# Float16 high and low parts in the MLP of an attention-plus-MLP kernel, from the third group on

## The chip, the core and the metric

The kernel runs on one core of a Trainium2 chip. Its time is that of one execution on the device in microseconds (us). The engines are named as in the profile: PE is TensorE (matrix products, with PEld its weight loads), DVE VectorE, ACT ScalarE, POOL GpSimd, and SP SyncE, which issues all transfers here.

## The reference

```python
# q, k, v: (8, 8, 576, 64); q and k about 0.67 in size, v 0.1
scores = 1/8 * q @ k^T;  rel = row - column
scores = where(0 <= rel < 128, scores - slope[head] * rel, -1e9)
attn   = softmax(scores);  y = attn @ v
x = y with the heads side by side: (4608, 512)
h = x @ w_in            # w_in: (512, 2048)
g = h / (1 + exp(-h))
out = g @ w_out         # w_out: (2048, 512)
```

q, k, v and out are float32, the weights float64. The kernel keeps close to float32 by splitting each MLP operand into a high and a low part and summing three products: high by high, high by low, low by high.

## The kernel before, in words

The 4608 rows are 36 blocks `i` of 128; a block has two passes `p` of four heads each. Two of the reference's batches make one of the kernel's four batches of nine blocks, with one scale for v. Four blocks are a group of 512 rows, nine groups `g`, counted from 0. While PE does the MLP of group g, it also does the attention of the next group's rows.

The order is written out by hand. A position counts half-slices of the MLP: the slice `f` of a group (16 of them, 128 of the 2048 columns each; `n` = 16 g + f) is two halves of the first product (`gemm1`, tile h) and two of the second (`gemm2`, tile o), so a group has 64 positions. Twelve matmuls of 512 columns belong to each product of a slice. The second product runs one slice behind the first. `put(position, function)` adds work to a position; all engines take their instructions in that order, each in its own queue. `at(p)` is the position at which pass p begins (`scores`); after it come `row_max`, `exps`, `p_hi` and `p_lo` (which split the softmax's numerator), a transposing transfer (`hl`), 13 to 15 positions later `attend`, and then `normalize`, `x_hi` and `x_lo`, which leave x as float16 high and low parts.

Between the products stand `act1` (ACT, tanh), `act2` (DVE), `act3` (ACT, gh: the high part) and `act4` (gl: the low part; POOL, and DVE in a group's last slice). MLP operands are float32r. x comes back through a transposing transfer (`x_dma`, tile xt, float16), and at the end of a group `turn_over` has `x_parts` write it out as float32r xh (ACT) and xl (DVE), 512 columns at a time. In group 0 ACT and DVE also split the float64 weights into high and low float32r parts (`w_split1` to `w_lo`). `vscale_load` and `vscale_reduce` find the largest |v| of the next batch, and `vscale_finish` turns it into a power of two: a reduction on DVE, a transpose on PE, small operations on one row, and a broadcast matmul on PE.

PSUM tiles of scores and of the attention's result share two buffers (`a`), so an `attend` waits until `row_max` has read scores of the buffer it takes.

Of the kernel before, what the change touches and what calls it, by code (L numbers as in the profile page):

```python
# [6 lines left out]
F32 = mybir.dt.float32  # L7
# [61 lines left out]
def tile_window_attention_then_silu_mlp(ctx, tc, qk, v, w_in, w_out, base8, out):  # L69
# [9 lines left out]
    ones16 = const.tile([P, 2 * P], BF16, name="ones16")  # L79
# [5 lines left out]
    def weight(kind, f):  # L85

        key = f"{kind}{f}"
        if key not in weights:
            shape = [P, NCC, P] if kind in ("wih", "wil") else [P, DM]
            if key in LAST:  # L90
                weights[key] = pool.tile(shape, F32R, tag=key, bufs=1, name=key)
            else:
                weights[key] = const.tile(shape, F32R, name=key)
# [27 lines left out]
    def keep_warm(n):  # L121

        for _ in range(n):
            nc.tensor.matmul(
                spare["a"][:, 4 * (D + 1) :], ones16[:, :P], ones16[:, : DM - 4 * (D + 1)],
                start=True, stop=True, skip_group_check=True,
            )

# [11 lines left out]
    def vscale_reduce(b, i):  # L140
        t = vred[b][i]
        if i == 0:
            vred[b]["m"] = pool.tile([P, VCH], F32, tag="vm", name=f"vmx{b}")
        m = vred[b]["m"][:, i : i + 1]
        if b == 0 and i < GT:
            rvs[i] = t

        if b == 0 and i % 2:
            nc.vector.tensor_reduce(m, t, axis=AX.X, op=ALU.max, apply_absolute_value=True)
        else:  # L150
            junk = pool.tile([P, DM], F32, tag="gt", name=f"vj{b}_{i}") if b == 0 else t
            nc.scalar.activation(junk, t, AF.Abs, accum_out=m)

    def vscale_finish(b, stage):
        r = vred[b]
        if stage == 0:
            r["col"] = col = pool.tile([P, 3], F32, tag="vcol", name=f"vcol{b}")
            nc.vector.tensor_reduce(col[:, 0:1], r["m"], axis=AX.X, op=ALU.max)
        elif stage == 1:
            col = r["col"]  # L160
            ps = ps_of(next_tag("misc"), f"vt{b}")
            nc.tensor.transpose(ps[:1, :P], col[:, 0:1], ident)
            c = col[:1, 1:2]
            nc.vector.tensor_reduce(c, ps[:1, :P], axis=AX.X, op=ALU.max)
# [4 lines left out]
            nc.vector.tensor_scalar(c.bitcast(I32), c.bitcast(I32), -1, 268 << 23, op0=ALU.mult, op1=ALU.add)
        else:  # L170
            ps = ps_of(next_tag("misc"), f"vs{b}")
            nc.tensor.matmul(ps[:, 0:2], ones[:1, :], r["col"][:1, 1:3], start=True, stop=True)
            vsc[b] = pool.tile([P, 2], F32, tag="vsc", bufs=3, name=f"vsc{b}")
            nc.vector.tensor_copy(vsc[b], ps[:, 0:2])
            del vred[b]


    ks, qs, rvs, st = {}, {}, {}, {}
# [190 lines left out]

    def x_dma(i):  # L370

        if i % 2 == 0:
            xt[i, "t"] = pool.tile([P, 2, 2 * NCC, P], F16, tag="big", name=f"xt{i}")
        nc.sync.dma_start_transpose(xt[i & -2, "t"][:, i % 2], xt[i].rearrange("p a c -> p (a c)"))

# [39 lines left out]

    def act3(n):
        gt = gact[n]
        gh = pool.tile([P, TG], F32R, tag="gh", name=f"gh{n}")
        gl = pool.tile([P, TG], F32R, tag="gl", name=f"gl{n}")
        nc.scalar.copy(gh, gt)  # L420
        gact[n] = (gh, gl, gt)

    def act4(n):
        gh, gl, gt = gact[n]
        (nc.vector if n % NF == NF - 1 else nc.gpsimd).tensor_sub(gl, gt, f32(gh))  # L425
# [16 lines left out]
    def gemm2(n, half):  # L442
        g, f = divmod(n, NF)
        for ti in (2 * half, 2 * half + 1):
# [4 lines left out]
            hi, lo = weight("woh", f), weight("wol", f)  # L449
            seq = [(gh, hi), (gh, lo), (gl, hi)]  # L450
            for i, (a, w) in enumerate(seq):
                nc.tensor.matmul(  # L452
# [2 lines left out]
                )  # L455

    def store(g, ti):
        tag, bufs = ("x", 4) if g == NG - 1 or ti > 1 else ("io", 2)
        ot = pool.tile([P, DM], F32, tag=tag, bufs=bufs, name=f"ot{g}_{ti}")
        if ti % 2:  # L460
            nc.vector.tensor_scalar_mul(ot, ops[ti], 0.5 / W_SCALE**2)
        else:
            nc.scalar.mul(ot, ops[ti], 0.5 / W_SCALE**2)
        nc.sync.dma_start(out[g * TG + ti * P : g * TG + (ti + 1) * P, :], ot)


# [47 lines left out]
    for p in range(NPAIR):  # L514
# [42 lines left out]
        if q == 0:  # L557
# [4 lines left out]
                put(n - 2, load_v, i)  # L562
            put(a - 3, v_hi, i)
            put(a - 2, v_lo, i)
    for b in range(1, NBB):
        n = at(2 * NBLK * b)
        for i in range(VCH):
            put(n - 54 + 5 * i, vscale_load, b, i)
            put(n - 50 + 5 * i, vscale_reduce, b, i)
        for x in range(3):  # L570
            put(n - 6 + 2 * x, vscale_finish, b, x)

    pos = [at(0)]

# [29 lines left out]
            fn(*a)  # L604

    with tc.manual_schedule():
        nc.gpsimd.memset(ones16, 1.0)
        nc.gpsimd.memset(ones, 1.0)
        make_identity(nc, ident)
# [105 lines left out]
```

## Time and profile before

| what | value |
|---|---|
| runs | 1033.23, 1029.6, 1031.43 us; median 1031.43 |
| the profiled execution | 1031.76 us, span 1030.0 us, mean granted PE clock 0.986 |
| busy: PE, DVE, ACT, POOL | 987.2, 572.2, 463.2, 217.9 us |
| chain that ended last | PE 79%, DVE 10%, transfers 4% |
| mean of `act1` (L409), `act2` (L414), `act3` (L420), `act4` on POOL (L425) | 597, 686, 615, 1310 ns |
| mean of a 512-column matmul from start to end | 395 to 414 ns (they overlap) |

A row of the timeline is start, duration, engine, line, operation, out<-in, shapes, count, and in brackets the idle time of the engine just before it with what ended it. A group's row has the count, then busy time and mean in ns, then idle time before. A row of a window has its length, then busy time and count of PE, PEld, DVE, ACT and POOL, the granted clock, the share of the transfer engines and GB/s.

### The profile page before, as it was taken

Reading aid. Unit: us, or ns where it says so; the run is one execution under the profiler, and the core shown is the slowest. Engines: PE = TensorE matmul, PEld = TensorE weight load, DVE = VectorE, ACT = ScalarE, POOL = GpSimd, SP = SyncE. Lnnn points to the kernel's source line nnn. Section 1 sums busy time; section 2 is a strip of 40 time slices with the busy share of each in tenths; the row PEclk is TensorE's granted clock in tenths of the full one; section 3 lists DMA queues with packets and bytes.
Section 4 is the critical chain, followed back from the end, with each engine's and each line's share of the span. In section 5 each row is a group of like instructions: output and inputs, shape, how many; then the busy total and the mean of one; then the engine's idle time right before and its main releaser. Section 6 shows DMA issues by size and latency. Waiting matters only on the chain.

```text
span 1030.0 us, 16885 instructions
## 1 busy us (share of the span) xinstructions
PE 987.2 (96%) x6374; PEld 782.8 (76%) x6374; DVE 572.2 (56%) x1399; ACT 463.2 (45%) x968; POOL 217.9 (21%) x188
## 2 busy tenths in 40 slices
PE   7978898999999998999999999999999999999998
PEld 5756676777777776777777778777777777787886
DVE  4889998555555555555555555554655555543111
ACT  4666676334454445334443355433444453333222
POOL 3022222122212221222122211222122212222221
PEclk8999999899999999999999999999999999999999
DMA  7278987333353446433353336433433444321001
GB/s 229 69 188 197 252 219 208 84 75 79 82 116 85 100 113 152 82 62 83 76 120 76 90 102 154 102 72 72 107 79 77 78 123 82 59 35 52 1 1 41
DMA packets 201073, 104.92 MB, mean 102 GB/s; under 512 B 168224, under 2 KB 176416, under 8 KB 200992
## 3 DMA queue, kind: packets, MB, share of 16 engines
q1 hardware_dynamic: 200992, 103.84, 42.7%
q8 instruction: 50, 0.82, 0.3%
q14 instruction: 31, 0.25, 0.1%
HBM read 54.00 MB, written 9.44 MB: 62 GB/s over the span
## 4 chain that ended last, share of the span: by engine, by line
PE 79%; DVE 10%; DMA 4%; issue 3%; ACT 2%; SPq 1%; POOL 0%; ACTq 0%; DVEq 0%; POOLq 0%
PE h L402 34%; PE o L452 32%; PE sp L227 6%; PE av L317 4%; DMA wr<-w_in 2%; DVE wm L492 2%; DVE t L247 1%; DVE wm L487 1%; DMA vm<-v 1%; DVE xl L390 1%; DVE hr L271 1%; DVE gt L414 1%; DVE wol L506 1%; DVE wil L506 1%; PE pt L289 1%
## 5 line engine op out<-in xcount | busy, mean ns | idle before, releaser
L425 POOL TENSOR_TENSOR gl<-gt,gh 128x512 fp32r<-128x512 f32 x135 | 176.9, 1310 | 776.4 <-ACT gh L420 683.5
L409 ACT ACTIVATE gt<-h 128x512 f32<-128x512 f32 x144 | 85.9, 597 | 445.3 <-PE h L402 445.2
L414 DVE SCALAR_TENSOR_TENSOR gt<-gt,h 128x512 f32<-128x512 f32 x144 | 98.8, 686 | 268.3 <-ACT gt L409 268.3
L402 PE MATMUL h<-xh,wih 128*128 128x512 f32 x576 | 238.2, 414 | 4.8 <-ACT xh L367 3.8
L452 PE MATMUL o<-woh,gh 128*128 128x512 f32 x576 | 230.9, 401 | 1.4 <-ACT gh L420 1.4
L452 PE MATMUL o<-woh,gl 128*128 128x512 f32 x576 | 229.9, 399 | 2.0 <-POOL gl L425 1.9
L452 PE MATMUL o<-wol,gh 128*128 128x512 f32 x576 | 228.4, 397 | 0.0
L402 PE MATMUL h<-xl,wih 128*128 128x512 f32 x576 | 227.5, 395 | 0.2 <-DVE xl L368 0.2
L402 PE MATMUL h<-xh,wil 128*128 128x512 f32 x576 | 227.6, 395 | 0.0
L271 DVE SCALAR_TENSOR_TENSOR hr<-t,hr 128x512 f16<-128x512 f32 (+1 forms) x128 | 121.0, 945 | 75.4 <-ACT hr L266 75.0
L402 PEld LDWEIGHTS h<-xh,wih 128*128 128x128 f32 x576 | 108.6, 189 | 32.6 <-ACT xh L367 4.0
L452 PEld LDWEIGHTS o<-woh,gl 128*128 128x128 f32 x576 | 109.0, 189 | 29.9 <-POOL gl L425 3.7
L452 PEld LDWEIGHTS o<-woh,gh 128*128 128x128 f32 x576 | 109.4, 190 | 27.0 <-ACT gh L420 2.3
L452 PEld LDWEIGHTS o<-wol,gh 128*128 128x128 f32 x576 | 109.3, 190 | 25.8
L402 PEld LDWEIGHTS h<-xh,wil 128*128 128x128 f32 x576 | 108.9, 189 | 25.0
L402 PEld LDWEIGHTS h<-xl,wih 128*128 128x128 f32 x576 | 109.0, 189 | 20.5 <-DVE xl L368 0.5
L257 ACT ACTIVATE t<-t,mx 128x256 f32<-128x256 f32 (+1 forms) x288 | 120.6, 487 | 7.3 <-DVE mx L247 7.0
L420 ACT CAST gh<-gt 128x512 fp32r<-128x512 f32 x144 | 88.5, 615 | 53.6 <-DVE gt L414 51.8
L247 DVE CUSTOM_DVE_ANT_0 t<-sp,tab 128x256 f32<-128x256 f32 (+1 forms) x288 | 101.5, 404 | 14.8 <-PE sp L227 8.4
L357 DVE TENSOR_TENSOR x<-xs,x 128x256 f16<-128x256 f32 x64 | 74.3, 1160 | 48.7 <-ACT x L351 48.7
L227 PEld LDWEIGHTS sp<-k,q 64*128 64x128 f32 x1088 | 68.5, 190 | 27.0 <-issue 26.1
L317 PEld LDWEIGHTS <-hl 128*128 128x128 f16 x1632 | 55.4, 98 | 38.9 <-issue 34.6
(68 smaller groups left out, 681.4 us busy)
## 6 DMA issues: line engine op xcount, KB each, us to landing
q<-qk SPq DMA_DIRECT2D x36, 256.0 KB, 3.0
k<-qk SPq DMA_DIRECT2D x36, 256.0 KB, 3.2
vm<-v SPq DMA_DIRECT2D x36, 256.0 KB, 3.7
out<-ot SPq DMA_DIRECT2D x36, 256.0 KB, 2.8
wr<-w_in SPq DMA_DIRECT2D x16, 512.0 KB, 4.0
wr<-w_out SPq DMA_DIRECT2D x16, 512.0 KB, 3.9
rv<-v SPq DMA_DIRECT2D x32, 256.0 KB, 3.0
hl<-hr SPq DMA_TRANSPOSE x128, 3.1
```

The lines of the kernel that those rows point to most:

```text
L227: nc.tensor.matmul(sp[h][:, u, o], qs[i][rows, 2 * q + u], ks[i - 1 + o][rows, 2 * q + u], start=True, stop=True, skip_group_check=True,)
L247: nc.vector.tensor_tensor_reduce(out=t[:, h, 2 * P - n :], in0=st[p]["sp"][h][:, u, o].rearrange("p o c -> p (o c)"), in1=tab[:, 4 * q + 2 ...
L257: nc.scalar.activation(x, x, AF.Exp, bias=st[p]["mx"][:, 2 * u + h : 2 * u + h + 1], scale=-1.0)
L271: nc.vector.scalar_tensor_tensor(out=hr[:, 1], in0=t[:, :, 2 * P - n :], scalar=PSCALE, in1=hr[:, 0], op0=ALU.mult, op1=ALU.subtract)
L317: nc.tensor.matmul(av[:, 2 * u + h, : rhs.shape[-1]], lhs, rhs, start=(n == 0), stop=(n == len(seq) - 1), skip_group_check=True,)
L357: nc.vector.tensor_sub(xt[i][:, 1, cols], st[p]["x"], xt[i][:, 0, cols])
L402: nc.tensor.matmul(hps[n], w[:, cc], x, start=(half == 0 and i == 0), stop=(half == 1 and i == len(seq) - 1), skip_group_check=True,)
L409: nc.scalar.activation(gt, hps[n], AF.Tanh, scale=0.5 / W_SCALE)
L414: nc.vector.scalar_tensor_tensor(out=gt, in0=gt, scalar=1.0, in1=hps[n], op0=ALU.add, op1=ALU.mult)
L420: nc.scalar.copy(gh, gt)
L425: (nc.vector if n % NF == NF - 1 else nc.gpsimd).tensor_sub(gl, gt, f32(gh))
L452: nc.tensor.matmul(ops[ti], a[:, t], w, start=(f == 0 and i == 0), stop=(f == NF - 1 and i == len(seq) - 1), skip_group_check=True,)
```

## The change

From group 2 on the first product, and from group 3 on the second, take float16 high and low parts instead of float32r.

- Weights: `w_stat` (ACT, one square with a sum for each of 32 weight tiles, positions 66 to 97) and `vscale_finish` (now also for weights, positions 100 to 102) give one power of two for each product; `conv1` (ACT), `conv2` and `conv3` (DVE) write each weight tile's float16 parts, w_in at positions 106 to 168, w_out at 172 to 234.
- x: `gemm1` moves the columns of the transposed tiles xt straight into PE, in group 2 from two tiles (two matmuls of 256 columns), later from one (512 columns). `x_parts` stays for groups 0 and 1 alone. `x_unit` makes one scale for a group with rows of two batches.
- gh and gl: `act3` scales by 2^-25 to float16; `act4` is on DVE in these groups. `act1` and `store` take their scale from a tile (`mlp_scales`).
- Maxima of v: for batches 1 to 3 all on DVE (before on ACT), and earlier: finished at positions 52 to 54, 180 to 182 and 308 to 310 (before 60 to 64, 204 to 208, 348 to 352).
- The matmuls that keep PE's clock up before the MLP take the identity instead of ones.

```diff
+IN16, OUT16 = 2, 3
+CUT = 2.0**-25
+STATS, CONV_IN, CONV_OUT = 66, 106, 172
...
-        if b == 0 and i % 2:
+        if b > 0 or i % 2:
             nc.vector.tensor_reduce(m, t, axis=AX.X, op=ALU.max, apply_absolute_value=True)
...
+    def w_stat(which, f):
...
+        nc.scalar.activation(
+            junk, f32(w_parts(f, which)[0]), AF.Square, accum_out=vred["w", which]["m"][:, f : f + 1]
+        )
...
+        if n // NF >= IN16:
+            g, w = n // NF, w16[0, f]
+            for cc in (2 * half, 2 * half + 1):
+                seq += [(0, 0, cc), (0, 1, cc), (1, 0, cc)]
+            for i, (wp, xp, cc) in enumerate(seq):
...
+                c = xp * NCC + cc
+                if g > IN16:
+                    moves = [(hps[n].rearrange("p (t c) -> p t c", t=GT), xt[g, "g"][:, :, c])]
+                else:
+                    moves = [
+                        (hps[n][:, k * P : (k + 2) * P].rearrange("p (t c) -> p t c", t=2), xt[g * GT + k, "t"][:, :, c])
+                        for k in (0, 2)
+                    ]
+                for k, (o, x) in enumerate(moves):
+                    nc.tensor.matmul(o, w[:, wp, cc], x, start=start and k == 0, stop=stop, skip_group_check=True)
+            return
...
+        if n // NF >= OUT16:
+            nc.vector.scalar_tensor_tensor(out=gl, in0=gt, scalar=CUT, in1=gh, op0=ALU.mult, op1=ALU.subtract)
+            return
         (nc.vector if n % NF == NF - 1 else nc.gpsimd).tensor_sub(gl, gt, f32(gh))
...
-        more = n // NF + 1 < NG
+        more = n // NF + 1 < IN16
...
-        tag, bufs = ("x", 4) if g == NG - 1 or ti > 1 else ("io", 2)
+        tag, bufs = ("x", 4) if ti > 1 else ("io", 2)
...
+        nc.scalar.activation(out16, f32(hi), AF.Copy, scale=wsc["w", which][:, 0:1])
...
+        r = pool.tile([P, DM], F32, tag="io", name=f"wr16_{which}_{f}")
...
+        nc.vector.scalar_tensor_tensor(
+            out=r, in0=f32(hi), scalar=wsc["w", which][:, 0:1], in1=out16, op0=ALU.mult, op1=ALU.subtract
+        )
...
+            out=low16, in0=f32(w_parts(f, which)[1]), scalar=wsc["w", which][:, 0:1], in1=r, op0=ALU.mult, op1=ALU.add
...
+    for k in range(2 * NF):
+        put(STATS + k, w_stat, k % 2, k // 2)
+    for x in range(3):
+        for which in range(2):
+            put(STATS + 2 * NF + 2 + x, vscale_finish, ("w", which), x)
+    for which, n in enumerate((CONV_IN, CONV_OUT)):
+        for f in range(NF):
+            for k, fn in enumerate((conv1, conv2, conv3)):
+                put(n + SLICE * f + (k if which or f else 0), fn, which, f)
...
-        n = at(2 * NBLK * b)
+        n = at(2 * GT * (NBLK * b // GT)) + 2
         for i in range(VCH):
             put(n - 54 + 5 * i, vscale_load, b, i)
             put(n - 50 + 5 * i, vscale_reduce, b, i)
         for x in range(3):
-            put(n - 6 + 2 * x, vscale_finish, b, x)
+            put(n + x, vscale_finish, b, x)
```

Three places in the engines' queues follow, each as it stood before and as it stands now; a row is line, operation, out<-in.

ACT in group 1, slices 23 and 24 in the program's count (gt and gh are `act1` and `act3`, t is `exps`, hr is `p_hi`), before:

```order
L409 ACTIVATE gt23_2778<-h23_2758 128x512
L257 ACTIVATE t21_0_2765<-t21_0_2765,mx21_2756 128x256 x2
L257 ACTIVATE t21_1_2781<-t21_1_2781,mx21_2756 128x256 x2
L266 ACTIVATE hr21_0_2796<-t21_0_2765 128x512
L420 CAST gh23_2798<-gt23_2778 128x512
L266 ACTIVATE hr21_1_2809<-t21_1_2781 128x512
L409 ACTIVATE gt24_2854<-h24_2813 128x512
```

ACT at the same slices now (wj is `w_stat`):

```order
L487 ACTIVATE gt23_2836<-h23_2814 128x512
L308 ACTIVATE t21_0_2821<-t21_0_2821,mx21_2810 128x256 x2
L163 ACTIVATE wj0_13_2844,stat0_2388<-wih13_1951 128x512
L308 ACTIVATE t21_1_2839<-t21_1_2839,mx21_2810 128x256 x2
L317 ACTIVATE hr21_0_2856<-t21_0_2821 128x512
L163 ACTIVATE wj1_13_2858,stat1_2402<-woh13_2084 128x512
L500 CAST gh23_2860<-gt23_2836 128x512
L317 ACTIVATE hr21_1_2871<-t21_1_2839 128x512
L163 ACTIVATE wj0_14_2875,stat0_2388<-wih14_2049 128x512
```

Two squares now stand between `act1` and `act3` of slice 23.

DVE at the end of group 5, slice 95 (gt and gl are `act2` and `act4`, t and mx are `row_max`, v2 is `v_lo`, hr is `p_lo`), before:

```order
L414 SCALAR_TENSOR_TENSOR gt95_7669<-gt95_7669,h95_7649 128x512
L425 TENSOR_TENSOR gl95_7674<-gt95_7669,gh95_7673 128x512
L390 TENSOR_SCALAR xl_119<-xt24_6866,vsc2_4808 128x4x128 x2
L390 TENSOR_SCALAR xl_119<-xt26_7407,vsc2_4808 128x4x128
L390 TENSOR_SCALAR xl_119<-xt26_7407,vsc3_7253 128x4x128
L247 ISA t57_1_7685,mx57_7647<-sp57_0_7637,tab_65 128x256
L247 ISA mx57_7647 128x1
L247 ISA t57_1_7685,mx57_7647<-sp57_1_7638,tab_65 128x256
L247 ISA mx57_7647 128x1
L209 SCALAR_TENSOR_TENSOR v2_69<-rv28_7498,vsc3_7253,v1_68 128x512
```

DVE at the same place now:

```order
L492 SCALAR_TENSOR_TENSOR gt95_8113<-gt95_8113,h95_8093 128x512
L508 SCALAR_TENSOR_TENSOR gl95_8117<-gt95_8113,gh95_8116 128x512
L298 ISA t57_1_8121,mx57_8091<-sp57_0_8081,tab_65 128x256
L298 ISA mx57_8091 128x1
L298 ISA t57_1_8121,mx57_8091<-sp57_1_8082,tab_65 128x256
L298 ISA mx57_8091 128x1
L260 SCALAR_TENSOR_TENSOR v2_68<-rv28_7942,vsc3_6962,v1_67 128x512
```

The four xl operations are gone, so the row maxima and `v_lo` follow gl at once.

PE in group 1, the second product of slice 24, before:

```order
L452 MATMUL o1_1_2417<-woh8_104,gl24_2871 128x512
L452 MATMUL o1_2_2429<-woh8_104,gh24_2870 128x512
L452 MATMUL o1_2_2429<-wol8_105,gh24_2870 128x512
L452 MATMUL o1_2_2429<-woh8_104,gl24_2871 128x512
L452 MATMUL o1_3_2433<-woh8_104,gh24_2870 128x512
L452 MATMUL o1_3_2433<-wol8_105,gh24_2870 128x512
L452 MATMUL o1_3_2433<-woh8_104,gl24_2871 128x512
L402 MATMUL h26_2943<-xh_118,wih10_110 128x512
```

PE at the same place now (vtw and vsw are the transposes and the broadcasts of the weights' `vscale_finish`):

```order
L540 MATMUL o1_1_2429<-woh8_103,gl24_2941 128x512
L176 MATMUL vtw0_3002<-ident_64,vcolw0_2987 1x128
L176 MATMUL vtw1_3011<-ident_64,vcolw1_2989 1x128
L540 MATMUL o1_2_2443<-woh8_103,gh24_2940 128x512
L540 MATMUL o1_2_2443<-wol8_104,gh24_2940 128x512
L540 MATMUL o1_2_2443<-woh8_103,gl24_2941 128x512
L540 MATMUL o1_3_2447<-woh8_103,gh24_2940 128x512
L540 MATMUL o1_3_2447<-wol8_104,gh24_2940 128x512
L540 MATMUL o1_3_2447<-woh8_103,gl24_2941 128x512
L192 MATMUL vsw0_3035<-vcolw0_2987,ones_66 128x2
L192 MATMUL vsw1_3039<-vcolw1_2989,ones_66 128x2
L479 MATMUL h26_3043<-xh_117,wih10_109 128x512
```

Transposes and broadcasts stand six matmuls apart in PE's queue, with DVE's small operations in between.

More of the change, by code (lines that the diff above doesn't have):

```diff
@@ L78, in tile_window_attention_then_silu_mlp @@
     ones = const.tile([P, P], F32, name="ones")
-    ones16 = const.tile([P, 2 * P], BF16, name="ones16")
+    ident16 = ident.bitcast(BF16)
     v1 = const.tile([P, VSLOTS, H, D + 1], F16, name="v1")
@@ L89, in weight @@
             shape = [P, NCC, P] if kind in ("wih", "wil") else [P, DM]
[L90 to L93, printed above, removed]
+            weights[key] = pool.tile(shape, F32R, tag=key, bufs=1, name=key)
         return weights[key]
@@ L370, in x_dma @@
     def x_dma(i):
-        if i % 2 == 0:
+        g = i // GT
+        if g > IN16 and i % GT == 0:
+            whole_x = pool.tile([P, GT, 2 * NCC, P], F16, tag="xh" if g % 2 else "xl", bufs=1, name=f"xt{i}")
+            for k in range(0, GT, 2):
+                xt[i + k, "t"] = whole_x[:, k : k + 2]
+            xt[g, "g"] = whole_x
+        elif g <= IN16 and i % 2 == 0:
             xt[i, "t"] = pool.tile([P, 2, 2 * NCC, P], F16, tag="big", name=f"xt{i}")
@@ L448, in gemm2 @@
             t = slice(ti * P, (ti + 1) * P)
-            hi, lo = weight("woh", f), weight("wol", f)
+            if g < OUT16:
+                hi, lo = weight("woh", f), weight("wol", f)
+            else:
+                hi, lo = w16[1, f][:, 0], w16[1, f][:, 1]
             seq = [(gh, hi), (gh, lo), (gl, hi)]
@@ L506, in w_lo, with conv1, conv2, conv3 @@
         nc.vector.tensor_sub(lo, wraw.pop((f, which))[1], f32(hi))
+    w16, rest = {}, {}
+    def conv1(which, f):
+        hi = w_parts(f, which)[0]
+        if which:
+            w16[1, f] = t = pool.tile([P, 2, DM], F16, tag=f"wih{f}" if f else f"wil{NF - 1}", bufs=1, name=f"wo16_{f}")
+            parts = [t[:, k] for k in range(2)]
+        elif f:
+            w16[0, f] = t = pool.tile([P, 2, NCC, P], F16, tag=f"wil{f - 1}", bufs=1, name=f"wi16_{f}")
+            parts = [t[:, k].rearrange("p a b -> p (a b)") for k in range(2)]
+        else:
+            parts = [pool.tile([P, DM], F16, tag="xs", bufs=2, name=f"wi16_{k}_{f}") for k in range(2)]
+        rest[which, f] = parts
+        out16 = parts[0]
+        nc.scalar.activation(out16, f32(hi), AF.Copy, scale=wsc["w", which][:, 0:1])
+    def conv2(which, f):
+        hi, out16 = w_parts(f, which)[0], rest[which, f][0]
+        r = pool.tile([P, DM], F32, tag="io", name=f"wr16_{which}_{f}")
+        rest[which, f].append(r)
+        nc.vector.scalar_tensor_tensor(
+            out=r, in0=f32(hi), scalar=wsc["w", which][:, 0:1], in1=out16, op0=ALU.mult, op1=ALU.subtract
+        )
+    def conv3(which, f):
+        out16, low16, r = rest.pop((which, f))
+        nc.vector.scalar_tensor_tensor(
+            out=low16, in0=f32(w_parts(f, which)[1]), scalar=wsc["w", which][:, 0:1], in1=r, op0=ALU.mult, op1=ALU.add
+        )
+        if not which and not f:
+            w16[0, f] = t = pool.tile([P, 2, NCC, P], F16, tag="wih0", bufs=1, name="wi16_0")
+            for k, part in enumerate((out16, low16)):
+                nc.scalar.copy(t[:, k].rearrange("p a b -> p (a b)"), part)
     plan = {}
@@ L564, in tile_window_attention_then_silu_mlp @@
             put(a - 2, v_lo, i)
+    for k in range(2 * NF):
[7 more added lines that the diff above has]
+                put(n + SLICE * f + (k if which or f else 0), fn, which, f)
+    for g in range(1, NG):
+        put(at(2 * GT * g) + 10, x_unit, g)
+        if g >= IN16:
+            put(g * SLICE * NF - 2, mlp_scales, g)
     for b in range(1, NBB):
-        n = at(2 * NBLK * b)
+        n = at(2 * GT * (NBLK * b // GT)) + 2
         for i in range(VCH):
@@ L606, in tile_window_attention_then_silu_mlp @@
     with tc.manual_schedule():
[L607 removed]
+        make_identity(nc, ident)
         nc.gpsimd.memset(ones, 1.0)
[L609 removed]
         ps_of("a", "warm")
```

76 lines of the change are left out of this document (60 added, 16 removed).

## The prediction

> **What bounds the kernel now.** I read the page first (busy time, the chain that ended last), then the chain in order of time, then the timeline of TensorE (PE) at steady places and at its stalls, and last the busy time by stretches.
>
> ```profile
> PE 987.2 (96%) x6374; PEld 782.8 (76%) x6374; DVE 572.2 (56%) x1399; ACT 463.2 (45%) x968; POOL 217.9 (21%) x188
> PE 79%; DVE 10%; DMA 4%; issue 3%; ACT 2%; SPq 1%; POOL 0%; ACTq 0%; DVEq 0%; POOLq 0%
> ...
> 945.49 2.75 PE h L402 x12
> 948.24 2.79 PE o L452 x12
> ```
>
> PE is busy nearly always and carries 79% of the chain; the rest is short stalls. The MLP runs back to back: twelve matmuls of 512 columns from 945.49 to 948.24 are 229 ns a step (I take 230) in the first product, and 2.79/12 = 232.5 ns in the second. The question is what sets that step.
>
> ```profile
> 411.47:414.89 3.42, 3.42 (x8) 2.74 (x9) 1.89 (x2) 2.19 (x5) 1.28 (x1) 0.50 0.14 37
> ...
> 412.06 0.63 PE L452 MATMUL o<-woh,gh 128*128 128x512 f32 x1
> 412.49 0.63 PE L452 MATMUL o<-wol,gh 128*128 128x512 f32 x1
> ...
> L402 PEld LDWEIGHTS h<-xh,wih 128*128 128x128 f32 x576 | 108.6, 189 | 32.6 <-ACT xh L367 4.0
> L317 PEld LDWEIGHTS <-hl 128*128 128x128 f16 x1632 | 55.4, 98 | 38.9 <-issue 34.6
> ...
> 5.54 2.97 PE L124 MATMUL warm<-ones 128*128 128x252 bf16 x26
> ...
> L124 PE MATMUL av<-ones 128*128 128x252 bf16 x64 | 9.7, 282 | 0.0
> ...
> 523.37 0.90 PE L317 MATMUL av<-v,hl 128*128 128x65 f16 x24
> 524.10 0.48 PE L402 MATMUL h<-xh,wih 128*128 128x512 f32 x1
> 524.41 0.39 PE L402 MATMUL h<-xl,wih 128*128 128x512 f32 x1
> ...
> 529.55 0.50 PE L402 MATMUL h<-xh,wih 128*128 128x512 f32 x1
> 529.89 0.39 PE L402 MATMUL h<-xl,wih 128*128 128x512 f32 x1
> ```
>
> The first row is a stretch at a granted clock of 0.50 (the column before the last two). There the same matmul steps 0.43 us: the columns alone, which would be half, 0.213-0.215 us, at full clock. The full-clock step is 15 to 20 ns longer, so something that does not scale with the columns binds it; the nearest candidate is the weight load of 189 ns, which starts as the previous matmul starts. A 16-bit load takes 98 ns and overlaps: 24 attention matmuls of 65 columns, each with its load, take 524.10 - 523.37 = 0.73 us, 30 ns each. And 26 matmuls of 252 columns in bf16 step (2.97 - 0.282)/25 = 107.5 ns. The line through both is 0.412 ns a column; 260 columns on from 252 it gives 215 ns at 512.
>
> **The change, part by part.** A group of 512 rows has 64 positions, some 1.4 to 1.7 us each.
>
> *Matmuls in float16.* First product, groups 2 to 8: 7 x 192 = 1344 steps, 230 to 215 ns: -20.2 us. Second, groups 3 to 8: 6 x 192 = 1152, 232.5 to 215: -20.2. Group 2 moves x in halves of 256 columns, two steps of about 108 ns, no difference. Together **-40.3**; bounds -47 (213 ns and below) and 0 (the step stays). I take the line, since it rests on 16-bit matmuls with their loads.
>
> *The first load after attention.* After 24 attention matmuls the next h matmul starts 0.31 us ahead of its follower (524.10), after scores 0.34 (529.55), against 0.23: 0.08 + 0.11 us waiting for a 32-bit load. 48 of each lie before a float16 matmul: -9.1 at most, 0 at least; **-7**.
>
> *x straight from its transfer.* Each turn of a group loses the four ACT and four DVE conversions (`x_parts`).
>
> ```profile
> 289.05 1.67 DVE L390 TENSOR_SCALAR xl<-xt,vsc 128x512 fp32r<-128x512 f16 x4
> ...
> 290.14 0.40 PE L452 MATMUL o<-woh,gl 128*128 128x512 f32 x1
> ...
> 291.21 0.28 PE L317 MATMUL av<-v,hl 128*128 128x65 f16 x4 [0.67 <-DVE mx L247]
> 291.31 0.75 DVE L209 SCALAR_TENSOR_TENSOR v<-rv,vsc,v 128x512 f16<-128x512 f32 x1
> ...
> 292.12 0.76 PE L317 MATMUL av<-v,hl 128*128 128x64 f16 x20 [0.64 <-DVE v L209]
> ```
>
> DVE spends 1.67 us on xl, then does row maxima and `v_lo`, for which PE waits 0.67 and 0.64 us (1.6 us from start to start). Six turns look so: -9.8 at most. PE will come 0.4 us earlier, and at the turns into groups 2 and 3 the weight conversions stand in that place (one of them reuses an output buffer of `io` and must wait for its store): **-6.5**. Late next could be x itself, which now must have landed as a whole:
>
> ```profile
> 929.19 1.23 SPq L374 DMA_TRANSPOSE xt<-x  x1
> ...
> xt<-x SPq DMA_TRANSPOSE x32, 3.1
> ```
>
> The last tile of group 8 is sent at 929.19 and lands in about 3.1 us; PE has some 30 matmuls of 0.23 us still to do, 7 us, so 4 us are left, and 0.5 us less of them in float16.
>
> *The scales of batch 1.* `vscale_finish` moves from positions 60-64 of group 0 to 52-54.
>
> ```profile
> 181.55 0.37 PE L162 MATMUL vt<-ident,vcol 128*1 128x128 f32 x1 [4.31 <-DVE vcol L158]
> ...
> 187.77 0.50 PE L402 MATMUL h<-xh,wih 128*128 128x512 f32 x1
> ```
>
> PE stood 4.3 us, from 177.2, because the reduction is queued on DVE behind xl, which waited for x; then the clock halved, and group 1 began at 187.77. Its xl, ahead of the reduction, was done before 181.55. Without the stall PE's last 12 matmuls and an attention block (2.8 + 0.7 us) end at 180.7, so group 1 can begin by 181.6: 0 to -6; **-5**, since PE will stand about a microsecond for xl.
>
> *A late load of v.* The loads for batch 2 move from positions 156-196 to 126-166.
>
> ```profile
> 404.78 0.97 SPq L137 DMA_DIRECT2D vm<-v  x1
> ...
> 408.78 0.63 ACT L152 ACTIVATE vm<-vm 128x512 f32<-128x512 f32 x1 [3.19 <-issue]
> ...
> 410.06 0.50 PE L452 MATMUL o<-woh,gh 128*128 128x512 f32 x1 [1.41 <-ACT gh L420]
> ...
> 411.47 0.79 PE L452 MATMUL o<-woh,gl 128*128 128x512 f32 x1 [0.68 <-POOL gl L425]
> ```
>
> A load put at position 191 was issued behind the output stores of the turn on SP's queue; ACT's reduction stood 3.2 us for it, PE then 1.41 + 0.68 us, and eight matmuls ran at half clock (8 x 0.2 = 1.6). In the new places the load at the turn stands ahead of the stores: 0 to -4.4; **-3**. Should one be late again, it is DVE that stands, since the reduction moves there.
>
> *What is added,* against the room on ACT and DVE:
>
> ```profile
> 60.00:140.00 80.00, 70.35 (x465) 54.40 (x463) 74.64 (x171) 56.95 (x117) 19.65 (x13) 0.98 0.88 221
> 188.00:242.00 54.00, 53.89 (x323) 42.37 (x323) 27.42 (x72) 20.85 (x47) 12.05 (x11) 1.00 0.40 93
> 294.20:401.70 107.50, 106.20 (x705) 84.39 (x704) 60.48 (x148) 49.79 (x109) 22.56 (x19) 1.00 0.47 106
> ...
> L271 DVE SCALAR_TENSOR_TENSOR hr<-t,hr 128x512 f16<-128x512 f32 x17 | 16.3, 961 | 12.1 <-ACT hr L266 12.1
> ...
> L357 DVE TENSOR_TENSOR x<-xs,x 128x256 f16<-128x256 f32 x8 | 9.7, 1207 | 6.9 <-ACT x L351 6.9
> ...
> L152 ACT ACTIVATION_READ_ACCUMULATOR vm<-vm 128x1 f32 x7 | 1.3, 189 | 0.0
> ...
> 7.52 0.69 DVE L149 TENSOR_REDUCE vmx<-vm 128x1 f32<-128x512 f32 x1 [0.31 <-DMA vm<-v]
> ...
> 183.63 0.27 DVE L164 TENSOR_REDUCE vcol<-vt 1x1 f32<-1x128 f32 x1
> ...
> 184.46 0.14 DVE L169 TENSOR_SCALAR vcol<-vcol 1x1 int32<-1x1 int32 x1
> ```
>
> The columns after the length are PE, load, DVE, ACT, POOL. Group 0 is DVE's (74.6 of 80 us): nine reductions of 0.69 us come to it from ACT, 0 to +6.2; **+3**. The 32 squares (`w_stat`) cost ACT 0.63 + 0.19 us each, 26 us at one per position into some 53 us where ACT works 20.9: nearly 90%. Queued behind them are `act1` and `act3`, and PE has 5.6 us (24 matmuls) between a product and its use, of which `act1` to `act4` need 3.2 by the means in the table above: 0 to +8, **+3**. The weights' scales: seven one-row operations for each product (from 183.63 to 184.60 five take 0.97 us, so some 2.7 for both) lie between a transpose and a matmul of PE only one position of 1.4 us apart: +1 to +5, **+3**; batches 2 and 3 get the same spacing, 0 to +3, **+2**. The conversions: 32 ACT scalings (0.6 us, hidden) and 64 DVE operations at 0.69 to 0.96 us, 44 to 61 us, spread over positions 106 to 235, and 18 reductions, 12 us. Group 2 is the tightest: about 60 + 22 + 6 - 2 = 86 of 102 us on DVE, still below group 0's 93%, where PE waits. 0 to +15 (a fifth of the 73 us, were they moved to the path at group 0's density); **+5**, nearer the free end, as one operation stands at a position.
>
> *gl from POOL to DVE.*
>
> ```profile
> 169.01 0.42 DVE L357 TENSOR_TENSOR x<-xs,x 128x256 f16<-128x256 f32 x1
> ...
> 292.56 0.69 DVE L271 SCALAR_TENSOR_TENSOR hr<-t,hr 128x512 f16<-128x512 f32 x1 [0.49 <-ACT hr L266]
> ```
>
> 15 x 0.69 = +10.4 us of DVE per group. But L271 and L357 average 961 and 1207 ns, since many overlap POOL's subtraction; the two quoted, where POOL rests, take 0.69 and 0.42 us: 16 x 0.27 + 8 x 0.79 = -10.6. Cost **0**, hidden by DVE's idle 44%; if that cover goes, gl is what PE waits for.
>
> Sum: -40.3 - 7 - 6.5 - 5 - 3 + 3 + 3 + 3 + 2 + 5 = -45.8. The profiled execution took 1031.76 us (span 1030.0 and 1.8 around it; the median of the runs is 1031.43), so **986 us**.
>
> **Rivals.** *The step does not change* (1). If columns and a fixed cost set it whatever the type, the first two terms go: 1031.8 - 14.5 + 16 = 1033 us. For it: 229 to 232 ns is only 8% above the columns' time. Against: at half clock the extra is gone, and 252 bf16 columns show none. The Trainium skill, "TensorE: Matmul & The Clock Gate", section "Weight-path perf modes", speaks for it: the array takes one element per cell and clock whatever the width, and a weight load scales with columns and not bytes. By that rule the time is this rival's 1033; the trace disagrees on the load (189 against 98 ns).
>
> *DVE or ACT is crowded in groups 1 to 3* (2). With the added work's terms at their upper ends (6.2 + 8 + 5 + 3 + 15 = 37) and half the gains of turns and loads: -47 - 7 + 37, about 1015 us.
>
> *DVE becomes the bound there* (3), slower than before: if each added DVE operation moved the end as it may in group 0, 61 us of conversions and 27 x 0.69 = 19 of reductions stand against gains of 62: about 1050 us. That decides once DVE's room in groups 1 to 3 (44% of some 320 us, 140 us) were under the 73 us added, so the profile is against it; only bunching speaks for it.
>
> *Everything falls well* (4): the columns' step of 213 ns, turns and loads at their full gain, added work nearly hidden: -47 - 9 - 9.8 - 6 - 4.4 + 8 = -68, 964 us.
>
> A new wait of over 3 us would cost twice: the trace shows 0.50 of the clock after such stalls. The same page, section "What's actually happening", has the clock halved after an idle window of about 3.4 us; the half-clock stretch at 411.47 lasted 3.42, though the two waits before it sum to 2.1.
>
> **How the numbers follow.** Forecast (972 to 1004 us) 0.78, (1) 0.06, (2) 0.08, (3) 0.02, (4) 0.06. A measurement of this kernel tells 0.3% (3 us) from no change. (1) splits into a third each way; the others but (3) are faster: faster 0.94, same 0.02, slower 0.04. The range, 968 to 1006 us, takes in the ends of (4) and of (2).
>
> **What would show it.** Right: 16-bit h and o matmuls 214-217 ns apart with loads near 98 ns; a group from the fifth on 99 us long instead of 107; no wait of `av` at turns. Wrong: steps of 230 ns; DVE over 90% in group 2 with PE waiting on row maxima; a PE wait of over 3 us at the weights' scales, about position 100; half clock there.

## The result and the profile after

The changed kernel takes 986.13 us (median of 983.54 to 987.78) against 1032.33 us for the kernel before in the same series (1029.6 to 1034.64): a ratio of 0.9551 [0.9518, 0.9584], 46 us faster. The profiled execution took 983.54 us (span 981.8), the fastest of its four and 48.2 less than the one of before that the prediction was made against.

The page after, engines and the chain that ended last:

```profile
PE 943.0 (96%) x6572; PEld 581.3 (59%) x6572; DVE 625.8 (64%) x1599; ACT 481.9 (49%) x984; POOL 100.2 (10%) x97
PE 78%; DVE 12%; DMA 4%; ACT 3%; issue 2%; SPq 1%; POOL 0%; ACTq 0%; DVEq 0%; POOLq 0%
...
L474 PEld LDWEIGHTS <-wi 128*128 128x128 f16 x1536 | 143.6, 98 | 130.8 <-issue 2.2
```

PE bounds it as before, with 44 us less work; DVE has 54 us more and stays at 64%; weight loads in the first product take 98 ns where they took 189. The steady MLP in the timeline of PE, after:

```profile
512.83 1.46 PE L474 MATMUL h<-xt,wi 128*128 128x512 f16 x6
514.12 0.89 PE L368 MATMUL av<-v,hl 128*128 128x65 f16 x24
514.84 1.46 PE L474 MATMUL h<-xt,wi 128*128 128x512 f16 x6
...
519.92 2.76 PE L474 MATMUL h<-xt,wi 128*128 128x512 f16 x12
```

Twelve float16 matmuls reach from 519.92 to the end of the last one in 2.76 us; one alone lasts 0.38, so the step is (2.76 - 0.38)/11 = 216 ns. Six of them after an attention block take 1.46 us just like six ahead of it: the long first step is gone.

To see where the time went I cut each execution at the first matmul of the first product in each group. Lengths in us, from the timelines (the last column runs to the last matmul):

| group | 0 | 1 | 2 | 3 | 4 | 5 | 6 | 7 | 8 |
|---|---|---|---|---|---|---|---|---|---|
| before | 139.1 | 106.4 | 107.5 | 110.7 | 107.5 | 106.5 | 107.5 | 102.5 | 89.3 |
| after | 140.9 | 107.3 | 110.2 | 97.4 | 99.9 | 97.1 | 98.7 | 95.2 | 82.9 |

Groups 3 to 8 give 52.8 us; groups 0 to 2 cost 5.4. Group 2, where the first product is already in float16, is *longer* than before. There the chain of work runs through this place (timeline of all engines, then of the stretch that follows: length, then busy us and count of PE, PEld, DVE, ACT, POOL, then clock):

```profile
298.96 2.88 SPq L553 DMA_DIRECT2D out<-ot  x2
...
300.12 0.75 DVE L618 SCALAR_TENSOR_TENSOR wr<-wih,vscw,wi 128x512 f32<-128x512 f32 x1 [3.96 <-DMA out<-ot]
300.79 0.68 DVE L550 TENSOR_SCALAR ot<-o 128x512 f32<-128x512 f32 x1
301.39 0.15 DVE L386 TENSOR_SCALAR r<-av 128x4 f32<-128x4 f32 x1
...
302.31 0.42 DVE L395 TENSOR_TENSOR xs<-av,r 128x256 f32<-128x256 f32 x1
...
302.87 0.57 PE L278 MATMUL sp<-k,q 64*128 64x128 f32 x5 [3.47 <-DVE xs L395]
```

```profile
304.20:307.80 3.60, 3.60 (x21) 2.52 (x19) 3.42 (x12) 0.62 (x1) 1.30 (x1) 0.53 0.25 73
296.20:406.40 110.20, 105.09 (x901) 86.11 (x900) 86.47 (x196) 54.30 (x106) 23.28 (x19) 0.98 0.43 108
```

Read it from the top: `conv2` (L618) writes a tile of the ring `io`, whose two buffers are also the output tiles. The outputs of group 1 are just being stored, so DVE stands 3.96 us for a store. Behind it in DVE's queue are another output, then `normalize` (L386 to L395, with the last step of a conversion among its operations), which frees the PSUM buffer that PE's scores need: PE stands 3.47 us, and then the granted clock is 0.53 for 3.6 us. DVE is busy for 86.5 of this group's 110.2 us; the prediction had reckoned 86.

### The profile page after: what moved, and what is told of

The parts are those of the page before. It is cut to its first block, busy times and chain, and to the rows that moved or that the text cites. A ratio compares the mean times of both kernels' runs of the same rounds, so it can differ in the third digit from the quotient of the medians.

```text
span 981.8 us, 17277 instructions
## 1 busy us (share of the span) xinstructions
PE 943.0 (96%) x6572; PEld 581.3 (59%) x6572; DVE 625.8 (64%) x1599; ACT 481.9 (49%) x984; POOL 100.2 (10%) x97
## 4 chain that ended last, share of the span: by engine, by line
PE 78%; DVE 12%; DMA 4%; ACT 3%; issue 2%; SPq 1%; POOL 0%; ACTq 0%; DVEq 0%; POOLq 0%
PE o L540 32%; PE h L474 30%; PE sp L278 6%; PE h L479 4%; PE av L368 4%; DVE wm L581 2%; DVE t L298 1%; DVE wm L576 1%; DMA wr<-w_in 1%; DVE gt L492 1%; DMA wr<-w_out 1%; DVE hr L322 1%; DVE wol L595 1%; DVE v L260 1%; DMA hl<-hr 1%
## 5 line engine op out<-in xcount | busy, mean ns | idle before, releaser
L474 PE MATMUL h<-xt,wi 128*128 128x512 f16 (+1 forms) x1536 | 317.8, 354 | 0.0
L487 ACT ACTIVATE gt<-h,gsc 128x512 f32<-128x512 f32 x112 | 77.0, 688 | 318.5 <-PE h L474 316.4
L540 PE MATMUL o<-wo,gh 128*128 128x512 f16 x768 | 228.4, 379 | 0.0
L474 PEld LDWEIGHTS <-wi 128*128 128x128 f16 x1536 | 143.6, 98 | 130.8 <-issue 2.2
L540 PE MATMUL o<-wo,gl 128*128 128x512 f16 x384 | 145.6, 379 | 0.0
L510 POOL TENSOR_TENSOR gl<-gt,gh 128x512 fp32r<-128x512 f32 x45 | 62.1, 1379 | 287.4 <-ACT gh L500 230.9
L278 PE MATMUL sp<-k,q 64*128 64x128 f32 x1088 | 83.2, 289 | 4.6 <-DVE xs L395 4.1
L540 PE MATMUL o<-woh,gh 128*128 128x512 f32 x192 | 79.2, 413 | 0.7 <-DVE mx L298 0.4
L540 PE MATMUL o<-woh,gl 128*128 128x512 f32 x192 | 76.8, 400 | 1.6 <-POOL gl L510 1.6
L540 PE MATMUL o<-wol,gh 128*128 128x512 f32 x192 | 76.3, 398 | 0.0
```

The source lines that it names most:

```text
L278: nc.tensor.matmul(sp[h][:, u, o], qs[i][rows, 2 * q + u], ks[i - 1 + o][rows, 2 * q + u], start=True, stop=True, skip_group_check=True,)
L474: nc.tensor.matmul(o, w[:, wp, cc], x, start=start and k == 0, stop=stop, skip_group_check=True)
L487: nc.scalar.activation(gt, hps[n], AF.Tanh, scale=scale)
L540: nc.tensor.matmul(ops[ti], a[:, t], w, start=(f == 0 and i == 0), stop=(f == NF - 1 and i == len(seq) - 1), skip_group_check=True,)
```

## The experiments

Each was run beside the kernel before on the same chip, in four series on four chips. Times are medians, ratios are to the kernel before, with 95% intervals in brackets. The halves and the quarters were run once each, so they are read from the length of group 8.

**What sets the float32r step: halves.** In the kernel before, group 8's first product in two halves of 256 columns, so that each half has its own 32-bit weight load; and the same cut in the changed kernel.

```diff
+            cuts = (0, 2 * P) if n // NF == NG - 1 else (0,)
+            for k in cuts:
+                c = slice(k, k + TG // len(cuts))
+                nc.tensor.matmul(hps[n][:, c], w[:, cc], x[:, c], start=start and k == 0, stop=stop, ...)
```

> The kernel before, with the first product of the last group moved in halves of 256 columns, still float32r: 384 matmuls there instead of 192, same sums. If the 32-bit weight load sets the step (my theory), each half still takes about 230 ns: 192 x 230 = 44 us more, the last group 133 us instead of 89, about 1076 us. If columns and a fixed 17 ns set it, each half takes about 124 ns: 192 x 17 = 3 us more, about 1035 us.

> The changed kernel, with the first product of the last group moved in halves of 256 columns. If 16-bit loads lie wholly under the matmuls (my theory), a half takes 108 to 109 ns and the last group grows by at most 0.5 us: about 986.5 us. If a load of 98 ns and the 40 ns that a 32-bit load seems to need besides set it, a half takes 138 ns: 192 x (276 - 216) = 11.5 us more, about 998 us.

Measured: 1032.86 us for float32r halves (before: 1031.39), group 8 90.6 us instead of 89.3; 984.24 for float16 halves, group 8 83.3 instead of 82.9. PE and its weight loads in the float32r kernel:

```profile
961.88 0.39 PE L406 MATMUL h<-xh,wih 128*128 128x256 f32 x2
962.11 0.40 PE L406 MATMUL h<-xl,wih 128*128 128x256 f32 x2
...
961.99 0.30 PEld L406 LDWEIGHTS h<-xl,wih 128*128 128x128 f32 x2
```

A pair of halves steps 0.23 to 0.24 us (median of a half 119 to 120 ns), the same as one whole matmul. Two loads of 190 ns lie in 0.30 us: they overlap each other. Were a step bound by a load of 190 ns, each of the 192 matmuls would have taken 2 x 190 ns instead of 231, and group 8 29 us more. The float16 halves step 109 ns. So the weight load does not bind the step of 512 columns, and the reason that the prediction took as nearest falls; the size of the gain stands.

**Quarters.** The last run asked how far the loads do hide: the same cut into four of 128 columns, float32r.

> The kernel before, with the 512-column float32r matmuls of the first product in group 8 cut into four of 128 columns: 192 matmuls become 768, each with its own 32-bit weight load. The halves stepped 119 ns and the whole ones 231 to 233, a line of 0.44 ns a column and 7 ns a step. Theory now (float32r moves its columns 5% slower than float16, plus a few ns a step, and loads lie under the steps): 63 to 64 ns a quarter, four of them 253 ns instead of 231, group 8 longer by about 4 us (93 instead of 89.3), about 1035 us. Rival (a 32-bit load does occupy TensorE, for a time that the halves' 119 ns just covers): 110 to 119 ns a quarter, group 8 longer by 40 to 47 us, about 1075 us. If the extra were the columns alone, 58 ns a quarter and no change, 1031.

Measured: 1073.41 us (before: 1031.01), group 8 130.2 us, 40.9 longer. The rival of that expectation holds:

```profile
962.08 0.61 PE L406 MATMUL h<-xh,wil 128*128 128x128 f32 x4
962.52 0.61 PE L406 MATMUL h<-xh,wih 128*128 128x128 f32 x4
...
962.02 0.53 PEld L406 LDWEIGHTS h<-xh,wil 128*128 128x128 f32 x4
```

Four quarters take 0.44 to 0.45 us, 111 ns each, and the loads follow each other at the same distance (0.53 = 3 x 0.113 + 0.19). So with 128 columns each, about 111 ns pass from one load and matmul to the next; float16 pairs of a load and 65 columns take 30. Whether it is the load that needs 111 ns or a short float32r matmul is slow in itself, this run can't tell. A place in the kernel before points to the load. It is the first product after scores (timeline of all engines), where a load has no long matmul to lie under:

```profile
191.33 0.19 PEld L402 LDWEIGHTS h<-xh,wih 128*128 128x128 f32 x1
191.34 0.50 PE L402 MATMUL h<-xh,wih 128*128 128x512 f32 x1
...
191.44 0.19 PEld L402 LDWEIGHTS h<-xl,wih 128*128 128x128 f32 x1
191.67 0.39 PE L402 MATMUL h<-xl,wih 128*128 128x512 f32 x1
```

The next load starts 0.11 us after the first although a matmul of 512 columns stands between, and that matmul lasts 0.11 us longer than the one behind it. So about 110 ns is probably what the load itself needs; no run isolates it. The Trainium skill, "TensorE: Matmul & The Clock Gate", section "LDWEIGHTS (loading the stationary operand)", puts a load at its columns divided by 1.2 in ns, which makes 107 for 128 as an estimate, and the section "Weight-path perf modes" has a faster path for full 128-column weights that are not FP32: that fits 111 and 30. These 111 ns are only half of a 512-column step. What adds 15 to 17 ns there (231 or 233 against 216), and 10 at 256 columns (119 against 109), stays open.

**Everything but the types.** All the added work, with every matmul left in float32r.

```diff
-IN16, OUT16 = 2, 3
+IN16, OUT16 = 9, 9
```

(The converted weights go to one scratch tile that nothing reads, `x_parts` works at every turn, and gl stays on POOL.)

> The changed kernel with everything but float16: all groups stay in float32r, x is converted at every turn, gl stays on POOL; the squares, scales, conversions of the weights (into a spare buffer that nothing reads) and the moved maxima of v remain. By my sum the terms left are -5 - 3 + 3 + 3 + 3 + 2 + 5 = +8: about 1040 us, between 1034 and 1046. Rival: the gain comes from the moved work and not from the 16-bit step, then under 1010 us. Rival: the added work costs far more than 16 us and float16 hides it, then over 1050 us.

Measured: 1040.95 us, ratio 1.0094 [1.0078, 1.011]. The added work alone makes the kernel slower by nearly 10 us; float16 in PE and what comes with it is worth 55 us (1040.95 against 985.5 to 986.1). This kernel's groups 0 to 2 are 11.4 us longer than those of the changed one. Some 4 of it are the float16 steps and first loads of group 2, and 3.8 lie in group 0, whose length varies that much without any edit there (see below). Some may be this kernel's own, since one scratch tile lines the conversions up; that isn't shown.

**x copied at the turns.** As in the change, but float16 x goes through ACT and DVE copies (x 1.0) into a tile of 512 columns at each turn from group 2 on.

```diff
+        if i // GT >= IN16:
...
+            if part == 0:
+                nc.scalar.activation(x16[g, 0][:, :, cols], t[:, :NCC], AF.Copy, scale=1.0)
+            else:
+                nc.vector.tensor_scalar(x16[g, 1][:, :, cols], t[:, NCC:], 1.0, 1.0, op0=ALU.mult, op1=ALU.mult)
...
-                    moves = [(hps[n].rearrange("p (t c) -> p t c", t=GT), xt[g, "g"][:, :, c])]
+                moves = [(hps[n], x16[g, xp][:, cc])]
```

> The changed kernel with x copied at each turn by ACT and DVE into float16 tiles, as the float32r kernel did it, and moved from there; nothing else is changed (group 2 is moved in 512 columns too). If the copies caused the waits at the turns (my theory), each of six turns loses 1.1 to 1.6 us again: 993 to 996 us, with waits of av on row maxima and on v of 0.6 us each. Rival: with less work of POOL beside it DVE is early enough, then 985 to 988 us.

Measured: 991.15 us, ratio 0.9611 [0.9597, 0.9624]. The changed kernel itself was run once more, as the measure for the runs that follow:

> The changed kernel once more, as the measure for the runs beside it: 984 to 988 us, 0.955 of the kernel before.

Measured: 985.48 us, ratio 0.957 [0.9545, 0.9595]. The copies cost 4 to 7 us: 4 by the ratios, 5 to 6 by the medians, 6.6 by groups 1 to 7 of the profiled executions. That is less than the 993 to 996 us expected. At a turn PE waits for row maxima and `v_lo` behind the copies, and without copies only for `v_lo` (timelines of PE, first the kernel with copies at the turn into group 7, then the changed one at the turn into group 6; in both kernels these two turns have the same waits to 0.01 us):

```profile
804.24 0.28 PE L368 MATMUL av<-v,hl 128*128 128x65 f16 x4 [0.20 <-DVE mx L298]
805.15 0.76 PE L368 MATMUL av<-v,hl 128*128 128x64 f16 x20 [0.64 <-DVE v L260]
```

```profile
698.39 0.29 PE L368 MATMUL av<-v,hl 128*128 128x65 f16 x4
698.86 0.76 PE L368 MATMUL av<-v,hl 128*128 128x64 f16 x20 [0.19 <-DVE v L260]
```

**gl back on POOL.** With the scale POOL needs two operations.

```diff
-            nc.vector.scalar_tensor_tensor(out=gl, in0=gt, scalar=CUT, in1=gh, op0=ALU.mult, op1=ALU.subtract)
+                nc.gpsimd.tensor_scalar(gt, gt, CUT, 1.0, op0=ALU.mult, op1=ALU.mult)
+                nc.gpsimd.tensor_sub(gl, gt, gh)
```

(In a group's last slice gl stays on DVE.)

> The changed kernel with gl of the float16 groups on POOL again, in two operations (a scaling in place and a subtraction), the last slice of a group on DVE. By my sum moving it was worth nothing (10.4 us of DVE a group against 10.6): 985 to 988 us, with p_lo and x_lo back near 960 and 1200 ns. Rival: two POOL operations make gl 1.5 us later or more and PE waits for it: over 990 us. Rival: DVE's relief of 10 us a group shortens the turns: under 984 us.

Measured: 994.92 us, ratio 0.9627 [0.9603, 0.9651]. Groups 3 to 8 are 6.8 us longer together (578.0 against 571.2). The groups of instructions in that kernel:

```profile
L544 PE MATMUL o<-wo,gl 128*128 128x512 f16 x384 | 145.7, 379 | 5.6 <-POOL gl L512 5.6
...
L512 POOL TENSOR_TENSOR gl<-gt,gh 128x512 f16<-128x512 f32 x90 | 115.5, 1283 | 7.5
```

PE waits 5.6 us for gl in seven places: POOL's 634 + 1283 ns are longer than the room between the products allows in places. Another 3.8 us lie in its group 0 (144.7), which the edit does not touch; in the profiled executions whose edit leaves group 0 as it is, it takes anywhere from 140.7 to 144.7 us. What was expected of `p_lo` did not come true: it is not back near 960 ns. Over the whole execution, before and then with gl on POOL again:

```profile
L271 DVE SCALAR_TENSOR_TENSOR hr<-t,hr 128x512 f16<-128x512 f32 (+1 forms) x128 | 121.0, 945 | 75.4 <-ACT hr L266 75.0
```

```profile
L322 DVE SCALAR_TENSOR_TENSOR hr<-t,hr 128x512 f16<-128x512 f32 (+1 forms) x128 | 100.4, 784 | 62.7 <-ACT hr L317 62.4
```

**The added work, a piece at a time.** First no squares and no weights' scales (constants instead):

```diff
-    for k in range(2 * NF):
-        put(STATS + k, w_stat, k % 2, k // 2)
...
+            nc.gpsimd.memset(wsc["w", which][:, 0:1], 2.0 ** (6 + which))
```

> The changed kernel without the 32 squares and without the weights' scales on DVE and PE: the scales are constants, written at the start. My sum had 3 us for the squares and 3 for the scales: about 980 us. Rival, after the trace: group 1 became only 0.9 us longer than before although a turn of 1.6 us fell away, so squares and scales together cost 2.5 us at most: 983.5 to 986 us.

Measured: 983.71 us, ratio 0.9547 [0.9525, 0.9569]; group 1 105.5 us instead of 107.4 (the changed kernel again). 1.9 us, of which the changed kernel's waits show half, in group 1:

```profile
PE vsw L192 <- DVE vcolw L189: 0.9, 1, 0.9
```

That leaves about 1 us for the 32 squares. The intervals of the two totals overlap, so this rests on group 1, which takes 107.3 to 108.5 us in the executions that have squares and scales as in the change. Then the maxima of v for batches 1 to 3 back to ACT (every second one of batch 0 stays on DVE):

```diff
-        if b > 0 or i % 2:
+        if b == 0 and i % 2:
```

> The changed kernel with the maxima of v for batches 1 to 3 on ACT again, at the changed positions. My sum had 3 us for the nine reductions on DVE in group 0: 983 us. Rival A: in group 0 DVE is the bound, so each of the nine moves the end by its whole 0.68 us, 6 us less: 980 us. Rival B: the end of group 0 waits for x's transfer whatever DVE does, no change: 985 to 987 us.

Measured: 983.99 us, ratio 0.9545 [0.9521, 0.9568]; group 0 138.1 us instead of 141, group 1 108.4 instead of 107.4. In group 0 DVE has 4.5 us less to do, and 138.1 is below all seven executions that leave group 0 as it is (140.7 to 144.7). But group 1 takes 1.0 back and the intervals of the totals overlap, so a gain of 2 to 3 us rests on one execution. Then batch 1's loads, maxima and scale at their old positions:

```diff
-        n = at(2 * GT * (NBLK * b // GT)) + 2
+        n = at(2 * GT * (NBLK * b // GT)) + 2 if b > 1 else at(2 * NBLK * b)
...
-            put(n + x, vscale_finish, b, x)
+            put(n + x if b > 1 else n - 6 + 2 * x, vscale_finish, b, x)
```

> The changed kernel with loads, maxima and scale of batch 1 back at their old positions (the scale at 60 to 64). If the scale's transpose behind xl was worth 5 us (my sum), the wait of 4 us and the half clock come back: 990 to 992 us. Rival: the end of group 0 waits for x all the same, since the last weight part and with it x's transfers are late: 985 to 987 us.

Measured: 985.27 us, ratio 0.9562 [0.9541, 0.9583], not to be told from the changed kernel's 0.957. Its stall is back, and costs nothing that the times show; 5 us they would show (the end of group 0, first this kernel, then the changed one):

```profile
180.75 1.76 DVE L450 TENSOR_SCALAR xl<-xt,vsc 128x512 fp32r<-128x512 f16 x4
...
183.41 0.27 PE L176 MATMUL vt<-ident,vcol 128*1 128x128 f32 x1 [3.67 <-DVE vcol L172]
```

```profile
182.94 1.86 DVE L450 TENSOR_SCALAR xl<-xt,vsc 128x512 fp32r<-128x512 f16 x4
...
185.28 0.28 PE L368 MATMUL av<-v,hl 128*128 128x65 f16 x4 [1.01 <-DVE mx L298]
...
186.77 0.76 PE L368 MATMUL av<-v,hl 128*128 128x64 f16 x20 [1.21 <-DVE v L260]
```

With the scale early, x itself comes later: DVE's xl starts at 182.94 instead of 180.75, 1.6 us later counted from the start of group 0 (47.9 and 47.3). The scale's seven small operations now stand ahead of it, on a DVE that is busy for 126 of this group's 141 us, and x's transfers are sent later too (177.34 instead of 174.93); which of the two decides isn't isolated. PE then stands for the row maxima and `v_lo` behind xl instead of for the scale's reduction behind xl.

**The conversions out of the stores' way.** The wait of group 2 should go if no conversion that uses an `io` tile stands near a turn: w_in's from the sixth slice on four positions later, w_out's from the fifth on six.

```diff
-                put(n + SLICE * f + (k if which or f else 0), fn, which, f)
+                wait = (4 if f > 4 else 0) if which == 0 else (6 if f > 3 else 0)
+                put(n + SLICE * f + wait + (k if which or f else 0), fn, which, f)
```

> The changed kernel with the conversions from w_in's sixth and w_out's fifth weight tile on moved by 4 and 6 positions, past the output stores of the turns, whose buffers they share. In the trace DVE stood 4.0 us for a store at 296 us, PE 3.5 us behind it, and 3.4 us ran at half clock. If that wait is the cause, it goes: 3.5 + 1.7 = 5 us less, about 981 us. Rival: DVE meets the store's buffer at a later conversion, or the wait moves to another turn: 985 to 987 us.

Measured: 980.78 us, ratio 0.9501 [0.9481, 0.952], clear of the changed kernel's 0.957. Group 2 is 105.5 us instead of 110.2. The stretch of group 2 in that kernel:

```profile
297.00:402.50 105.50, 103.28 (x900) 84.98 (x899) 86.44 (x197) 54.53 (x106) 23.22 (x19) 1.00 0.45 113
```

DVE does the same 86.4 us of work there, now at 82% busy, PE's clock is 1.00, and no wait of DVE for a store is left in the trace there. One store, not the amount of work, made group 2 long. Last, with the steps of the scales two positions apart as well (the weights', and batches 1 to 3):

```diff
-            put(STATS + 2 * NF + 2 + x, vscale_finish, ("w", which), x)
+            put(STATS + 2 * NF + 2 * x, vscale_finish, ("w", which), x)
...
-            put(n + x, vscale_finish, b, x)
+            put(n - 2 + 2 * x, vscale_finish, b, x)
```

> The kernel with the conversions past the stores, and the three steps of every scale (of v and of the weights) two positions apart again instead of one. If the steps' waits of PE (1.3 us at 388 us, 1.1 us at 251 us in the trace) are real and not taken back elsewhere, 2 us less than with the conversions moved alone: about 979 us. Rival: no difference from that kernel, about 981 us.

Measured: 980.16 us, ratio 0.949 [0.947, 0.951]: the best version here, though not to be told from the one before by its time. Group 1 is 106.3 us instead of 108.1, group 2 104.3 instead of 105.5, group 0 143.2 instead of 141.7.

## Why the prediction was right, point by point

The forecast was 986.0 us. Its terms beside what the runs show:

| term | forecast, us | shown, us | from |
|---|---|---|---|
| float16 steps | -40.3 | -39.8 | 1344 x (231 - 216) + 1152 x (233 - 216) ns, median steps of both traces |
| first load after attention and scores | -7 | -8.6 | 48 x (82 + 97) ns, below |
| x straight | -6.5 | -4 to -7 | copies put back |
| batch 1's scale | -5 | about 0, within 2 | old positions |
| late load of v | -3 | about -4 | group 3 gains 13.3, group 5 9.4; no run isolates it |
| maxima of v on DVE | +3 | +2 to +3, one execution | maxima on ACT |
| squares and weights' scales | +6 | +1.9 in group 1 | left out |
| spacing of batches 2 and 3 | +2 | about +1 | two positions apart |
| conversions | +5 | +4.7 | moved from the stores |

- *The steps*: right in size. The 216 ns came out at the line through short 16-bit matmuls, to 1 ns. The reason that the prediction gave as the nearest candidate, the weight load of 189 ns, is wrong: such loads overlap each other and the columns, and halves with twice the loads take 1.3 us more in a group, not 29. What the prediction needed was only that 16-bit matmuls lie on the line; why float32r lies 7 to 8% above it is not settled.
- *The first load*: after attention the first step exceeded the usual one by 83 ns before (314 against 231) and by 1 now (217 against 216); after scores by 107 (338) and by 10 (226). The forecast left out part of it for caution, which was not needed. Here a 32-bit load has next to nothing to hide under: before, it starts 27 ns (median) ahead of its matmul after attention and 2 ns ahead after scores, and with the excess that makes 110 and 109 ns, as at 191.33.
- *x straight*: right, about as forecast. "No wait of `av` at turns" was too much: row maxima are in time, but a wait of 0.2 to 0.8 us for `v_lo` stays at the turns into groups 2 to 7.
- *Batch 1's scale*: the term that failed. The forecast took the stall of 4.3 us as lost time that an earlier reduction gives back, with group 1 beginning by 181.6. It begins at 188.8. The stall and its half clock are gone as forecast (granted clock 1.00 from 140 to 300 us), and yet group 0 is no shorter. The reduction only waited in the same queue as x's low part; PE now waits behind that low part itself, for row maxima and `v_lo`. The prediction had x done before 181.55, as in the trace of before; now its low part starts at 182.94. That moving the scale ahead of it made x later fits the two traces, but group 0 varies by more than these 1.6 us.
- *Squares and scales*: right that they hide, with too high a price (6 for 1.9). ACT was busy for 37.3 of the 50 us from 190 to 240, 75% and not the nearly 90% that the prediction reckoned, and PE waits there for neither `act1` nor `act3`.
- *Conversions*: the sum was right, its shape not. The forecast spread 5 us over 82 operations on a crowded DVE; what the runs show of it is one wait for a store, which the prediction named in passing (a conversion reuses an `io` buffer) and gave no price. This speaks against the rival of a crowded DVE too: DVE at 82% in group 2 does the same work without a delay once that wait is gone.
- *Spacing*: group 2 gives 1.2 us back with two positions, which fits batch 2's wait of 1.1 us; group 4 (batch 3) doesn't change.
- *gl*: forecast 0, out of two sums that cancel. Their premise is in the trace of before: in groups 3 to 8 `p_lo` takes 688 ns in the nine cases where POOL rests and 1010 ns in the 59 that its subtraction overlaps. In the changed kernel, where POOL rests, the mean over these groups is 684 ns for `p_lo` (963 before) and 419 for `x_lo` (1207 before): some 9 us less of DVE a group, near the 10.6 of the forecast. Over the whole execution, after:

```profile
L322 DVE SCALAR_TENSOR_TENSOR hr<-t,hr 128x512 f16<-128x512 f32 (+1 forms) x128 | 93.5, 748 | 21.4 <-ACT hr L317 21.4
```

The run with gl on POOL doesn't isolate this, since two operations there take longer than the one of before, and with them `p_lo` and `x_lo` take only 733 and 634 ns in groups 3 to 8. So it is not enough that POOL is busy; what else decides stays open. The run shows that in the changed kernel DVE is the better place.

The terms shown add up to between -46 and -50; the medians differ by 46.2 and the profiled executions by 48.2. The errors of +5 (batch 1) and -4 (squares and scales), with smaller ones, nearly cancel: that the total came out within 1 us is partly luck.

The remark that a stall of over 3 us costs twice was borne out at 302.87: 3.47 us standing, then 24 half matmuls (303.93 to 308.14) in 4.2 us instead of 2.6. The Trainium skill's rule on the clock ("TensorE: Matmul & The Clock Gate", section "What's actually happening": halved after an idle window of about 3.4 us) agrees with this place. At 411.47 before, half clock followed two waits of only 1.41 and 0.68 us, so a stall under 3 us can cost it too. Moving the conversions gave back 4.7 of those 5.1 us.

## What to carry to other kernels

Price a stall by what is late next and not by its length: one that stands in the same queue as the work that ends a stage gave nothing back here when it was removed. When extra work is fed into idle slots, look for the buffers it shares with transfers before counting its operations; one shared ring cost here what eighty operations did not. And a term measured on neighbours of the same type (a line through short 16-bit matmuls) can be exact while the mechanism told for it is wrong; test the mechanism apart.

## What the runs showed of the hardware

Float32r weight loads of 190 ns each overlap: they follow each other every 119 ns beside 256 columns and every 111 ns beside 128. With nothing to hide under, the next load starts 110 ns after the one before even beside 512 columns (191.33 and 191.44 before), so at 128 columns the load probably sets the pace. 16-bit loads of 98 ns follow each other every 30 ns. A float32r matmul is 15 to 17 ns longer in step than a float16 one at 512 columns (231 or 233 against 216), 10 ns at 256 (119 against 109). POOL's subtraction beside it made DVE's `p_lo` 1010 ns long instead of 688.
